# A second pair of output tiles by seven products, a visit moved ahead of a plain tile, and weight sums moved from GpSimd to VectorE

## The chip, the cores and the metric

The kernel runs on one core of one Trainium2 chip. The metric is the device time of one execution in microseconds (us). Engines are named as in the profile: PE is TensorE (matmuls; PEld its weight loads), DVE is VectorE, ACT is ScalarE, POOL is GpSimd, and SP is SyncE, which here only issues DMAs.

## The reference

Sigmoid attention without softmax, then a gated feed-forward block. Cut to what matters:

```python
# q, k, v: batch 8, heads 12, seq 448, head_dim 64
scores = scale * np.matmul(q, k.transpose(0, 1, 3, 2)) - np.log(S)
attn = 1.0 / (1.0 + np.exp(-scores))
x = np.matmul(attn, v)              # then (8 * 448, 12 * 64) = (3584, 768)
g = x @ w_gate                      # w_gate, w_val: (768, 1536)
silu = g * (1.0 / (1.0 + np.exp(-g)))
out = (silu * (x @ w_val)) @ w_out  # w_out: (1536, 768)
```

Inputs and output are float32; the kernel computes matmuls in 16-bit types with float32 accumulation.

## The kernel before

**Tiling.** Attention is cut into 24 blocks `n`, three for each batch and each of four heads. A block has seven chunks `c` of 64 keys for each head; `qk_tile` (L240) makes the scores of a chunk, `sig_tile` (L256, L259, on ACT) their sigmoid, and `pv` (L273) multiplies a whole block with v and gives two pieces `xT` of the feed-forward input. The feed-forward works on pairs of batches, `pb` 0 to 3. `ffn1(b, f)` (L314) makes 128 of the 1536 hidden columns for one batch, with the gate on ACT (L334) and DVE (L336, L340). In half of pair 2 and all of pair 3, `double` (L437) does two hidden columns of both batches at once by seven products of half-size blocks in place of eight (Strassen's scheme in Winograd's form). The second matmul gives seven output tiles of 128 rows for a pair.

**Output tiles, plain and grouped.** `ffn2(pb, m)` (L675) makes one output tile with 24 matmuls of 128x384; its two halves are evicted by ACT (L690) and DVE (L689). `ffn2_group(pb, g)` (L599) makes tiles `g` and `g + 3` together by seven products of six matmuls, 42 where two plain tiles need 48. It is a generator that stops after each product, in the order 1, 2, 6, 5, 7, 3, 4; the products alternate between the two banks of one PSUM tile and are evicted by DVE (L610, and L616, which adds to what is there), the first one by ACT (L623) when `act` is set. `ffn2_groups` runs several such generators in turn and calls one function of `extra` after each step.

**Sums.** The seven products need sums of blocks. `make_sums` takes row sums of the hidden tiles from a list (L532, DVE, 128x384). `w_sum(s, kind)` makes sums of `w_out`, eight in all (L498, DVE, 128x1152): kind 2 reads kind 3, and kind 4 reads kind 2. `fast_w(s, kind)` makes those of the first matmul's weights (L384): on DVE in one instruction when it is called from `extra` of a `double`, or on POOL in three of 128x384 when `early_w(2)` calls it, after POOL has made the sums of the last pair's input (L410 to L413). For `s` = 2 they are needed by the doubles from hidden column 6 on, for `s` = 3 from column 9 on.

**Order.** All is written in program order, and each engine runs its own instructions in that order. The list `units` holds `ffn1`, `double`, sums and output tiles with a planned length. `PACE` gives planned times for the attention blocks, and a visit (four or three chunks of a block; `attn_step`) is put ahead of the unit at which its time has come. After a visit, `plan` adds transfers: after chunk 4 of block `n` the casts of block `n + 2` (L191, POOL), their two DMA transposes (L198, SP), the load of its v (POOL) and the loads of q and k of block `n + 4` (SP). Stores of output tiles (L543) are issued by SP too, so all these stand in one queue; SP waits at the first whose data are not ready. POOL is often ahead of the program: it waits only for its own inputs.

**Memory.** Score tiles, gates, output tiles and groups take the four PSUM tiles of two banks in turn (`Banked`), whatever they are. Output tiles are staged in four buffers `osb`.

**Around the change.** At the end of pair 0 the order is: last gate `ffn1(1, 11)`, the last row sums, tile 6, the visit of block 8 (chunks 4 to 6), four `w_sum`, tile 0, three `w_sum`, tile 3, a visit of block 9, the group of tiles 1 and 4 (with the eighth `w_sum` after its second step), a visit, the group of tiles 2 and 5, a visit. In pair 3, six doubles follow each other with nothing between.

Of the kernel before, what the change touches and what calls it, by code (L numbers as in the profile page):

```python
# [13 lines left out]
MULT = mybir.AluOpType.mult  # L14
# [6 lines left out]
def kernel(  # L21
# [13 lines left out]
    B, H, S, D = q.shape  # L35
# [3 lines left out]
    NJ = H // 4  # L39
    NP = H // 2  # L40
    NF = DFF // 128
    NQ = B * NJ
    W2 = 2 * S
    LAST = B // 2 - 1
# [99 lines left out]
    def half_of(a):  # L144
        return a.rearrange("p a b s -> p (a b s)").bitcast(FP16)
# [160 lines left out]
    V, G = nc.vector, nc.gpsimd  # L306
# [51 lines left out]
    def fast_w(s, kind, i=None):  # L358

        js = slice(0, JT) if i is None else slice(i, i + 1)  # L360
        b11, b21 = wg16[s][:, 0::2][:, js], wg16[s][:, 1::2][:, js]
        b12, b22 = wv16[s][:, 0::2][:, js], wv16[s][:, 1::2][:, js]
        if (s, kind) not in gT:
            n = JT * FW * 128
            at = {3: 0, 2: 1, 4: 2}.get(kind)
            if kind == 1:
                t = wv16[s][:, 0::2]
            elif s == 0:
                t = half_of(stg_a)[:, at * n:(at + 1) * n]
            elif s == 1 and kind == 3:  # L370
                t = half_of(ramp_a)[:, 8 * FW * hw:8 * FW * hw + n]
            elif s == 1:
                t = pt_f[:, (at - 1) * n:at * n]
            elif s == 2:
                t = pt_f[:, (at + 2) * n:(at + 3) * n]
            else:
                t = osp.tile([128, DM], FP32, tag="osb", name=f"g{kind}").bitcast(FP16)[:, :n]
            gT[(s, kind)] = t if kind == 1 else t.rearrange("p (j n) -> p j n", j=JT)
        t = gT[(s, kind)][:, js]
        a, b, op = {  # L380
            3: (b22, b12, SUB), 1: (b12, b11, SUB), 2: (b22, gT.get((s, 1), gT[(s, kind)])[:, js], SUB),
            4: (b21, gT.get((s, 2), gT[(s, kind)])[:, js], SUB),
        }[kind]
        (V if i is None else G).tensor_tensor(out=t, in0=a, in1=b, op=op)  # L384
# [1 line left out]
    pt_f = pt_a.rearrange("p a b s -> p (a b s)")  # L386

    def early_w(s):
        for kind in (3, 1, 2, 4):
            for i in range(JT):  # L390
                fast_w(s, kind, i)

# [96 lines left out]
    def w_sum(s, kind):  # L489

        b11, b12 = wo16[2 * s][:, :, :hw], wo16[2 * s][:, :, hw:]
        b21, b22 = wo16[2 * s + 1][:, :, :hw], wo16[2 * s + 1][:, :, hw:]
        t = half_of(ramp_a)[:, len(wT) * FW * hw:(len(wT) + 1) * FW * hw].rearrange("p (f n) -> p f n", f=FW)
        wT[(kind, s)] = t
        a, b, op = {
            3: (b22, b12, SUB), 2: (wT.get((3, s)), b11, ADD), 1: (b12, b11, SUB), 4: (b21, wT.get((2, s)), SUB),
        }[kind]
        nc.vector.tensor_tensor(out=t, in0=a, in1=b, op=op)  # L498
# [35 lines left out]
    def store(engs, pb, m, osb, cols):  # L534

        for w in range(2):
            store_half(engs[w], pb, m, w, osb, cols)
# [119 lines left out]
        store((nc.sync, nc.scalar), *rows[1], oe, lo)  # L657

    def ffn2_groups(pb, gs, extra=()):
        gens = [ffn2_group(pb, g, len(gs) > 1) for g in gs]  # L660
        extra = list(extra)
        while gens:
            gens = [g for g in gens if next(g, g) is not g]
            if extra:
                extra.pop(0)()

    def ffn2(pb, m):
        D = Banked("o")

        head, tail = range(NF - 1), (NF - 1,)  # L670
        for half, fs in ((0, head), (1, head), (0, tail), (1, tail)):
            for f in fs:
                h = hT[(pb, f)].rearrange("p b s -> p (b s)")
                D.write(
                    nc.tensor.matmul(  # L675
                        out=D.t[:, half, :hw],
                        lhsT=h[:, m * 128:(m + 1) * 128],
                        rhs=wo16[f // FW][:, f % FW, half * hw:(half + 1) * hw],
                        start=(f == 0),
                        stop=(f == NF - 1),  # L680
                    ),
                    half,
                    uses=(pb, f),
                )
        osb = osp.tile([128, DM], FP32, tag="osb", name="osb")
        for half in range(2):
            o, i, by = osb[:, half * hw:(half + 1) * hw], D.t[:, half, :hw], 1.0 / hsc(pb)
            D.read(
                V.tensor_scalar(out=o, in0=i, scalar1=by, scalar2=None, op0=MULT) if half else  # L689
                nc.scalar.mul(out=o, in_=i, mul=by),  # L690
                half,
            )
        store((nc.sync, nc.sync), pb, m, osb, slice(0, DM))


    FU1, FU2, FU3, FU4 = 2.26, 3.9, 6.83, 7.85
    units = []
    f1_start, f1_end = {}, {}
    tt = 0.0
    for pb in range(B // 2):  # L700
        for b in (2 * pb, 2 * pb + 1):
            f1_start[b] = tt
            for f in range(NF):
                if f not in FAST.get(pb, ()):
                    if b or f > 2:
                        units.append((FU1, ffn1, (b, f)))
                    tt += FU1
            f1_end[b] = tt
        for f in FAST.get(pb, ())[::2]:
            extra = {  # L710
                (LAST - 1, 0): ((0, 4), (1, 2)), (LAST - 1, 2): ((1, 4),), (LAST, 0): ((3, 3), (3, 1)), (LAST, 2): ((3, 2), (3, 4)),
            }.get((pb, f), ())
            units.append((FU4, double, (pb, (f, f + 1), [lambda a=a: fast_w(*a) for a in extra])))
            tt += FU4
        o_units = [(0.0, make_sums, (99,))]
        if pb < LAST - 1:
            o_units.append((FU2, ffn2, (pb, C - 1)))
        if pb == 0:

            ts = [(0.0, w_sum, (s, kind)) for s in range(2) for kind in (3, 2, 1, 4)]  # L720
            o_units += ts[:4] + [(FU2, ffn2, (pb, 0))] + ts[4:7] + [(FU2, ffn2, (pb, 3))]
        ex = {(0, 1): (lambda: None, lambda: w_sum(1, 4)), (LAST - 1, 0): (keep_rest,)}
        gs = {0: ((1,), (2,)), LAST - 1: ((0, 1), (2,)), LAST: ((0, 1), (3,), (2,))}.get(pb, ((0,), (1,), (2,)))
        for g in gs:
            o_units.append((FU3 * len(g), ffn2_groups, (pb, g, ex.get((pb, g[0]), ()))))
        units += o_units
        tt += sum(u[0] for u in o_units)


    FIRST = f1_end[0] - 5.0  # L730
    PACE = ((2 * NJ, FIRST + 3.5), (3 * NJ, FIRST + 41.5), (3 * NJ + 2, FIRST + 60.5), (6 * NJ, f1_end[B - 5] - 1.0), (NQ, f1_end[B - 3] - 5.0))
    tiles = [(n, c) for n in range(NJ, NQ) for c in range(C)]
    visits = [tiles[:2], tiles[2:4]]
    for i in range(0, len(tiles), C):
# [2 lines left out]
    for grp in visits:  # L737
# [4 lines left out]
        else:  # L742
            at = n + (0.5 if c else 0.0)
            (n0, t0), (n1, t1) = [p for p in zip(PACE, PACE[1:]) if p[0][0] <= at][-1]
            vtime.append(t0 + (at - n0) / (n1 - n0) * (t1 - t0))
# [124 lines left out]
    early = [tile_of(0), tile_of(2)]  # L870
# [59 lines left out]
    for fn, args, how in seq:  # L930
# [28 lines left out]
        if fn is make_sums and hS and (LAST - 1, 4, FW - 1) in hS and (LAST, 3, 0) not in hS:  # L959
            G.tensor_copy(out=held[:, :1], in_=hS[(LAST - 1, 4, FW - 1)][:, :1])  # L960
            for j in range(NJ):
                for f in x_sums(LAST, j):
                    f()
            early_w(2)
# [32 lines left out]
```

## Time and profile before

| | |
|---|---|
| time, median of 4 runs | 404.52 us (404.25 to 407.78) |
| profiled execution, own time | 404.63 us |
| its span, first to last instruction | 402.9 us |
| granted TensorE clock, mean | 0.999 |
| PE busy | 391.7 us, 97% of the span |
| DVE, ACT, POOL busy | 270.0, 230.2, 104.4 us |
| plain output tiles (L675) | 4, 96 matmuls, 16.1 us on PE |
| sums on POOL for `s` = 2 (L384) | 12 instructions, 0.91 to 0.93 us each |

The page is of one execution. A line of the chain or of a timeline starts with the time from the start of the span and a length, both in us; "x" counts the instructions that were put together. In brackets stands how long the engine was idle before it, and what ended that. Lines are those of the kernel before. In the windows view, a stretch is followed by its length and the busy time of each engine in it.

### The profile page before, as it was taken

The numbers are of one execution on the slowest core, as the hardware profiler recorded it, in microseconds if no ns is written. First come the engines' busy times: TensorE is split into PE (matmuls) and PEld (weight loads), VectorE is DVE, ScalarE is ACT, GpSimd is POOL, SyncE is SP. The second block draws the span as 40 slices with busy tenths as digits, with TensorE's granted clock in tenths as the row PEclk, the third lists the DMA queues.
The fourth block names the chain that finished last, engine by engine and source line by source line (L and its number), as shares of the span: only waits on it lengthen the run. The fifth ranks groups of instructions, "written<-read, shape, count | busy, mean of one in ns | idle before, by whom it ended". The sixth has DMA issues, their size and how long they took to land.

```text
span 402.9 us, 8032 instructions
## 1 busy us (share of the span) xinstructions
PE 391.7 (97%) x3134; PEld 203.5 (51%) x3134; DVE 270.0 (67%) x509; ACT 230.2 (57%) x369; POOL 104.4 (26%) x146
## 2 busy tenths in 40 slices
PE   7799999999999999999999999999999999999995
PEld 3344545445555444444455554444555645555663
DVE  3637647798655555567774556888886588778753
ACT  5966885744444777777773547776654046756000
POOL 3628041352022232232200220000006950010700
PEclk9999999999999999999999999999999999999999
DMA  8999989998859997778716598000000530000055
GB/s 261 252 246 255 245 188 258 163 194 183 185 132 267 220 269 159 163 159 161 161 24 149 160 258 122 2 2 0 3 0 2 157 80 0 1 2 1 2 165 149
DMA packets 65286, 54.39 MB, mean 135 GB/s; under 512 B 35744, under 2 KB 61440, under 8 KB 65248
## 3 DMA queue, kind: packets, MB, share of 16 engines
q1 hardware_dynamic: 49744, 38.22, 37.8%
q0 software_dynamic: 15072, 15.34, 23.0%
q8 instruction: 24, 0.39, 0.4%
q10 hardware_dynamic: 432, 0.33, 0.3%
q14 instruction: 14, 0.11, 0.1%
HBM read 47.19 MB, written 11.01 MB: 144 GB/s over the span
## 4 chain that ended last, share of the span: by engine, by line
PE 92%; DMA 3%; DVE 2%; ACT 1%; issue 1%; SPq 0%; POOL 0%; DVEq 0%; ACTq 0%
PE ps_D L314 35%; PE ps_D L599 20%; PE ps_D L437 16%; PE ps_D L240 8%; PE ps_D L273 8%; PE ps_D L675 4%; DMA v<-in_v_dram 2%; DMA st<-in_q_dram 1%; DVE g L384 1%; PE ps_D L210 0%; DVE t L336 0%; DVE xT L288 0%; DVE xT L293 0%; ACT snap L447 0%; ACT s L334 0%
## 5 line engine op out<-in xcount | busy, mean ns | idle before, releaser
L259 ACT ACTIVATE pt_a<-ps_D 128x896 f16<-128x896 f32 x148 | 127.2, 918 | 54.8 <-PE ps_D L240 49.3
L314 PE MATMUL ps_D<-xT,wg 128*128 128x448 f16 x360 | 79.4, 353 | 0.6 <-DVE t L336 0.5
L314 PE MATMUL ps_D<-xT,wv 128*128 128x448 f16 x360 | 78.9, 352 | 0.0
L191 POOL CAST c<-stg_a 128x896 bf16<-128x896 f32 x40 | 37.5, 946 | 133.3 <-DMA stg_a<-in_q_dram 125.6
L336 DVE TENSOR_TENSOR t<-ps_D,s 128x448 f16<-128x448 f32 x60 | 37.4, 624 | 41.5 <-ACT s L334 40.5
L314 PEld LDWEIGHTS <-wg 128*128 128x128 f16 x360 | 32.3, 98 | 39.4 <-issue 13.6
L314 PEld LDWEIGHTS <-wv 128*128 128x128 f16 x360 | 35.1, 98 | 33.0 <-issue 0.4
L334 ACT ACTIVATE s<-ps_D 128x448 f16<-128x448 f32 x60 | 33.0, 550 | 26.5 <-PE ps_D L314 26.5
L240 PE MATMUL ps_D<-T,T 64*64 64x448 bf16 x644 | 44.1, 357 | 2.1 <-DVE T L216 1.0
L447 ACT ACTIVATE snap<-ps_D 128x448 f32<-128x448 f32 x54 | 28.0, 542 | 26.3 <-PE ps_D L437 24.7
L340 DVE SCALAR_TENSOR_TENSOR hT<-ps_D,t 128x448 f16<-128x448 f32 x60 | 37.5, 625 | 6.3
L273 PE MATMUL ps_D<-pt_a,v 64*64 64x448 f16 x672 | 35.9, 349 | 0.7 <-DMA v<-in_v_dram 0.7
L610 DVE TENSOR_SCALAR osb<-ps_D 128x384 f32<-128x384 f32 x43 | 24.0, 558 | 18.5 <-PE ps_D L599 17.8
L599 PEld LDWEIGHTS <-S 128*128 128x128 f16 x264 | 25.8, 98 | 17.1
L599 PE MATMUL ps_D<-ramp_a,S 128*128 128x384 f16 x198 | 33.6, 326 | 0.0
L616 DVE SCALAR_TENSOR_TENSOR osb<-ps_D,osb 128x384 f32<-128x384 f32 x36 | 20.0, 557 | 13.8 <-PE ps_D L599 13.8
L240 PEld LDWEIGHTS <-T 64*64 64x64 bf16 x644 | 14.9, 105 | 24.4 <-issue 17.9
L599 PEld LDWEIGHTS <-hT 128*128 128x128 f16 x204 | 19.6, 98 | 14.4 <-issue 1.8
L273 PEld LDWEIGHTS <-v 64*64 64x64 f16 x672 | 19.4, 107 | 13.5 <-DMA v<-in_v_dram 1.1
L288 DVE CAST xT<-ps_D 128x448 f16<-128x448 f32 x21 | 13.1, 625 | 18.9 <-PE ps_D L273 17.1
L293 DVE CAST xT<-ps_D 64x448 f16<-64x448 f32 x37 | 23.0, 622 | 0.8
L437 PE MATMUL ps_D<-xS,wv 128*128 128x448 f16 x108 | 23.4, 352 | 0.0
(110 smaller groups left out, 442.9 us busy)
## 6 DMA issues: line engine op xcount, KB each, us to landing
out_dram<-osb SPq DMA_DIRECT2D x52, 192.0 KB, 3.1
stg_a<-in_q_dram SPq DMA_DIRECT2D x18, 448.0 KB, 4.8
stg_a<-in_k_dram SPq DMA_DIRECT2D x18, 448.0 KB, 5.3
v<-in_v_dram POOLq DMA_DIRECT2D x24, 224.0 KB, 6.0
wg<-in_moe_w_gate_dram POOLq DMA_DIRECT2D x4, 576.0 KB, 12.4
wv<-in_moe_w_val_dram POOLq DMA_DIRECT2D x4, 576.0 KB, 12.7
wo<-in_moe_w_out_dram POOLq DMA_DIRECT2D x4, 576.0 KB, 9.5
stg_a<-in_q_dram POOLq DMA_DIRECT2D x3, 448.0 KB, 14.8
```

Source lines behind the costliest of these rows:

```text
L191: eng.tensor_copy(out=t.rearrange("p c h d -> p h c d"), in_=st.rearrange("p h (c d) -> p h c d", c=C))
L240: nc.tensor.matmul(out=sc[w * 64:(w + 1) * 64, h2, :S], lhsT=kt[r, w * 64:(w + 1) * 64], rhs=qt[r, :, w * 64:(w + 1) * 64], start=True, st ...
L259: nc.scalar.activation(out=pt, in_=sc[:, :, :S], func=SIGM, bias=sbias, scale=qkscale)
L273: nc.tensor.matmul(out=P[g:g + 64, h2, :S], lhsT=vt[r, h2, c * D:(c + 1) * D], rhs=pt[r, h2, :], start=(c == 0), stop=(c == C - 1),)
L314: nc.tensor.matmul(out=D.t[:, i, :S], lhsT=(wg16, wv16)[i][f // FW][:, pr, cs], rhs=xT[(b, pr)], start=(pr == 0), stop=(pr == NP - 1),),
L334: D.read(nc.scalar.activation(out=s16, in_=D.t[:, 0, :S], func=SIGM), 0)
L336: D.read(nc.vector.tensor_tensor(out=t1, in0=D.t[:, 0, :S], in1=s16, op=MULT), 0)
L340: nc.vector.scalar_tensor_tensor(out=hT[(b // 2, f)][:, b % 2, :], in0=D.t[:, 1, :S], scalar=hsc(b // 2), in1=t1, op0=MULT, op1=MULT),
L437: nc.tensor.matmul(out=D.t[:, bank, :S], lhsT=W(f, j), rhs=X(j), start=(start and j == 0), stop=(stop and j == JT - 1), skip_group_check=True,
L447: D.read(nc.scalar.mul(out=o, in_=D.t[:, bank, :S], mul=scale), bank)
L599: nc.tensor.matmul(out=D.t[:, bank, :hw], lhsT=l, rhs=B_(i), start=(first and i == 0), stop=(i == HF - 1), skip_group_check=True,),
L610: nc.vector.tensor_scalar(out=o, in0=D.t[:, bank, :hw], scalar1=1.0 / hsc(pb), scalar2=None, op0=MULT), bank
```

## The change

Tiles 0 and 3 of pair 0 become a group, run after tile 6 with its first eviction on ACT. Both halves of the plain tile 6 of pair 0 are evicted by ACT. Six of the eight `w_sum` stand before that group, four of them ahead of tile 6, and the other two are called after its third and fourth step. `PACE` gets two more points, so that the visit of block 8 (chunks 4 to 6) comes right after the last gate, ahead of the row sums and of tile 6; its other points are moved a little, and the order of all other visits stays the same. On the first weights, `early_w(2)` makes kinds 3 and 1 on POOL and no longer kinds 2 and 4; these go to DVE, as extras of the first and second double of pair 3. The extras for `s` = 3 move back: (3,3) from the first double to the second, (3,1) and (3,2) to the third, (3,4) to the fourth.

```diff
     def early_w(s):
-        for kind in (3, 1, 2, 4):
+        for kind in (3, 1):
             for i in range(JT):
                 fast_w(s, kind, i)
...
     def ffn2_groups(pb, gs, extra=()):
-        gens = [ffn2_group(pb, g, len(gs) > 1) for g in gs]
+        gens = [ffn2_group(pb, g, len(gs) > 1 or (pb, g) == (0, 0)) for g in gs]
...
-                V.tensor_scalar(out=o, in0=i, scalar1=by, scalar2=None, op0=MULT) if half else
+                V.tensor_scalar(out=o, in0=i, scalar1=by, scalar2=None, op0=MULT) if half and pb else
                 nc.scalar.mul(out=o, in_=i, mul=by),
...
             extra = {
-                (LAST - 1, 0): ((0, 4), (1, 2)), (LAST - 1, 2): ((1, 4),), (LAST, 0): ((3, 3), (3, 1)), (LAST, 2): ((3, 2), (3, 4)),
+                (LAST - 1, 0): ((0, 4), (1, 2)), (LAST - 1, 2): ((1, 4),), (LAST, 0): ((2, 2),),
+                (LAST, 2): ((2, 4), (3, 3)), (LAST, 4): ((3, 1), (3, 2)), (LAST, 6): ((3, 4),),
             }.get((pb, f), ())
...
         if pb == 0:
-
-            ts = [(0.0, w_sum, (s, kind)) for s in range(2) for kind in (3, 2, 1, 4)]
-            o_units += ts[:4] + [(FU2, ffn2, (pb, 0))] + ts[4:7] + [(FU2, ffn2, (pb, 3))]
-        ex = {(0, 1): (lambda: None, lambda: w_sum(1, 4)), (LAST - 1, 0): (keep_rest,)}
-        gs = {0: ((1,), (2,)), LAST - 1: ((0, 1), (2,)), LAST: ((0, 1), (3,), (2,))}.get(pb, ((0,), (1,), (2,)))
+            early = [(0.0, w_sum, a) for a in ((0, 3), (0, 2), (1, 3), (1, 2), (0, 1), (1, 1))]
+            o_units[1:1] = early[:4]
+            o_units += early[4:]
+        skip = lambda: None
+        ex = {
+            (0, 0): (skip, skip, lambda: w_sum(0, 4), lambda: w_sum(1, 4)), (LAST - 1, 0): (keep_rest,),
+        }
+        gs = {LAST - 1: ((0, 1), (2,)), LAST: ((0, 1), (3,), (2,))}.get(pb, ((0,), (1,), (2,)))
...
-    PACE = ((2 * NJ, FIRST + 3.5), (3 * NJ, FIRST + 41.5), (3 * NJ + 2, FIRST + 60.5), (6 * NJ, f1_end[B - 5] - 1.0), (NQ, f1_end[B - 3] - 5.0))
+    PACE = ((2 * NJ, FIRST + 3.5), (3 * NJ - 1, FIRST + 28.9), (3 * NJ - 0.5, f1_end[1] - 0.1), (3 * NJ, FIRST + 41.5), (3 * NJ + 2, FIRST + 59.5), (6 * NJ, f1_end[B - 5] - 1.0), (NQ, f1_end[B - 3] - 5.5))
```

## The prediction

> **What bounds the kernel now.** I read the page first (busy shares, the chain that ended last), then the chain in order of time at the two places that the change touches, then the timelines of VectorE (DVE), GpSimd (POOL) and SyncE (SP) there.
>
> ```profile
> PE 391.7 (97%) x3134; PEld 203.5 (51%) x3134; DVE 270.0 (67%) x509; ACT 230.2 (57%) x369; POOL 104.4 (26%) x146
> ...
> PE 92%; DMA 3%; DVE 2%; ACT 1%; issue 1%; SPq 0%; POOL 0%; DVEq 0%; ACTq 0%
> ```
>
> TensorE (PE) is busy for 97% of the span and holds 92% of the chain: a matmul taken away counts fully, and so does a wait put in front of one. The rest is read in two places. The first is the end of pair 0 (start, length, what):
>
> ```profile
> 97.46 3.90 PE ps_D L675 x24
> 101.36 0.69 PE ps_D L240 x12
> 102.06 7.91 PE ps_D L675 x48
> ...
> 112.17 6.93 PE ps_D L599 x42
> ```
>
> L675 is the plain product: tile 6 from 97.46, tiles 0 and 3 from 102.06. L599 is a pair of tiles made by seven products. The chain here is PE alone: 48 matmuls cost 7.91 us, 42 cost 6.93. The second place is the first double of the last pair:
>
> ```profile
> 325.86 2.95 DVE g L384
> ...
> 329.51 0.63 DVE v L473
> 330.14 0.04 issue
> 330.18 1.86 PE ps_D L437 x9
> ```
>
> Here the chain leaves PE: a weight sum on DVE (L384) takes 2.95 us, the eviction L473 is late behind it, and PE waits for that.
>
> **The change, part by part.** *1, the group.* Tiles 0 and 3 lose 48 matmuls and gain 42: 6.93 - 7.91 = **-0.98 us**, on the path.
>
> *2, the sums ahead of the group.* In the built order DVE runs the last row sums (L532), then six of the eight weight sums L498, (0,3), (0,2), (1,3), (1,2), (0,1), (1,1), and only then L616, the eviction of the group's second product. Their pace:
>
> ```profile
> 102.24 0.75 DVE L498 TENSOR_TENSOR ramp_a<-wo,wo 128x1152 f16<-128x1152 f16 x1
> 103.02 0.76 DVE L498 TENSOR_TENSOR ramp_a<-ramp_a,wo 128x1152 f16<-128x1152 f16 x1
> 103.70 0.75 DVE L498 TENSOR_TENSOR ramp_a<-wo 128x1152 f16<-128x1152 f16 x1
> ```
>
> A sum that reads its predecessor starts 0.78 after it, another 0.67 after. The row sums end at 100.38 (99.76 + 0.62 in the same view), as they will; six sums from 100.3 take 0.78 + 0.67 + 0.78 + 0.67 + 0.67 between their starts, so the last runs 103.9 to 104.6, and L616 (0.56) ends at 105.1. On PE the visit (0.69) now comes at 97.46, tile 6 (3.90) after it, the group at 102.05. Its fourth product in order writes the bank that L616 reads; it comes after 18 of 42 matmuls, 2.97 us on, at 105.0, and waits until 105.15: **+0.15**. The third product, at 104.0, needs sum (1,2), ready at 103.3. So visit and tile 6, 4.6 us of PE, are the cover of these sums, and it is used up: whatever delays DVE further between 98.4 and 104.6 reaches PE whole. Sums (0,4) and (1,4) run inside the group, some 0.5 us before its last product needs them.
>
> *3, the visit ahead of tile 6.* Its score tiles take PSUM tiles whose readers end by 96.7; tile 6 takes that of the last gate, read until 98.50 in the bank that it writes second: nothing waits. The visit carries two casts and a v load (POOL), two transposes and two loads (SP). POOL's order stays. On SP the transposes of block 10 and the loads of block 12 pass tile 6's two stores. SP, and then the casts on POOL that these loads release:
>
> ```profile
> 91.11 1.19 SPq L179 DMA_DIRECT2D stg_a<-in_k_dram  x1
> 102.35 1.19 SPq L543 DMA_DIRECT2D out_dram<-osb  x2
> 103.64 2.67 SPq L198 DMA_TRANSPOSE T<-c  x2
> 106.37 0.58 SPq L179 DMA_DIRECT2D stg_a<-in_q_dram  x1
> ```
>
> ```profile
> 110.44 0.93 POOL L191 CAST c<-stg_a 128x896 bf16<-128x896 f32 x1 [11.21 <-DMA stg_a<-in_q_dram]
> 111.97 0.94 POOL L191 CAST c<-stg_a 128x896 bf16<-128x896 f32 x1 [0.60 <-POOL c L191]
> ```
>
> SP stands from 92.3 to 102.35 at a store that waits for an eviction. With that store behind them, the transposes (cast by 90.5) go at 92.4, the loads at 95.1 and 95.8. From load to cast took 4.07 and 4.97 us here (issued 106.37 and 107.00), 5.18 and 6.53 for the two issued at 90.47 and 91.11. So the casts of block 12 move to 99.2-100.3 and 100.8-102.3, **into the sums of part 2**. What that costs, other rows show, POOL's and DVE's:
>
> ```profile
> 86.61 3.84 POOL L191 CAST c<-stg_a 128x896 bf16<-128x896 f32 x4
> ```
>
> ```profile
> 86.77 1.01 DVE L532 TENSOR_TENSOR S<-hT,S 128x384 f16<-128x384 f16 x1
> 87.70 1.08 DVE L532 TENSOR_TENSOR S<-hT 128x384 f16<-128x384 f16 x1
> ```
>
> Alone such a row sum takes 0.35. The five beside casts, from 71.7 to 90.7, took 1.43, 0.71, 1.01, 1.08 and 0.70: 0.64 lost in the mean, each to one cast. Bounds for one cast: nothing (the sum at 98.42 beside the cast of 97.64 took 0.37), and 1.08. A gain is excluded, as a cast gives DVE nothing. I take the mean, since these rows have the same cast and the same kind of sum: 2 x 0.64 = **+1.28**; ends 0 and 2.16.
>
> The Trainium skill (SBUF — State Buffer, "Who interferes with whom") says that a DVE instruction with two inputs in SBUF contends with a GpSimd instruction that reads SBUF, and that the one that issues second is blocked until the first has finished. That speaks against putting these sums under casts. By it a cast could cost its whole 0.93, the sum of the case then being 0.6 higher, near 405.0. The trace goes beyond the rule: the L384 of 325.86 was overtaken by two POOL sums that started after it.
>
> *4, two kinds of sums from POOL to DVE.* POOL's run of L384 (0.88 each) ends six instructions earlier, at about 322.9 instead of 328.2. In the first double DVE then has one sum of 0.75 with POOL idle in place of 2.95 + 0.75, and L473 is on time. The first double took 8.54 us on PE from start to start (322.77 to 331.31), the next 7.95 (to 339.26): **-0.59**; ends -0.43 (PE's bare idle time there) and -0.60. The second double keeps two sums. The third gets two (1.47 from their rows) ahead of its row sums: these end at 345.2 in place of 343.74, L473 starts at 345.13 instead of 344.80 and ends at 345.75, and its product comes at 346.07: hidden by 0.3; if that cover is gone it costs up to 0.3. The fourth double gets one sum, where DVE idled 0.67.
>
> *5, small parts.* Evictions: the group adds six on DVE (0.56 each) and takes three away, in a stretch with 3.8 us of DVE idle in 12.5; tile 6's second half goes to ScalarE, whose three evictions (0.49 each) end by 103.7, ahead of the third product at 104.0. The stores stay 14. Block 11's transposes still stand behind the first group's stores, at 120, and are read at 136. All at nothing.
>
> *Sum:* -0.98 + 0.15 + 1.28 - 0.59 = -0.14 us. The profiled execution took 404.63 (span 402.9 and 1.7 around it): 404.49; it stood 0.11 above the median of 404.52, so 404.4 for a median.
>
> **The rivals.** *A, the casts cost nothing:* they miss the sums (load 12 lands later than any row says), or DVE, which has its sums queued, holds POOL up instead. For it: the sum at 98.42. Against: six weight sums and six row sums leave no hole from 98.4 to 104.6, and both casts are due inside. Sum: -0.98 + 0.15 - 0.59 = -1.42: **403.1**. With one cast alone, 403.7.
>
> *B, slower: POOL keeps DVE out in a run.* At 325.86 a DVE sum of 0.75 waited through the rest of three POOL sums in a row, losing 2.19. If both casts and the v issue behind them run back to back (0.93 + 0.94 + 0.72), DVE loses 2.59: -0.98 + 0.15 + 2.59 - 0.59 = +1.17: **405.7**. It takes hold from a loss of 1.42 on, and needs the two landings within 0.9 of each other; against it, the last two pairs of casts lay 1.53 and 1.99 apart.
>
> *C, the change doesn't do what it says in the last pair:* the late row is the third double's, part 4 gives 0.3 back: 404.7.
>
> **How the numbers follow.** Forecast 0.50, its own range by the bounds of the cast from 0.35 each to 1.08 each: 403.8 to 405.3. A 0.30, B 0.15, C 0.05. The range takes in A with its bounds and the upper end of the forecast, up to B's edge: 403.0 to 405.5. One per cent, 4.0 us, is about what a measurement of this kernel can tell from no change; no case comes near it: faster 0.02, same 0.96, slower 0.02.
>
> **What would show it.** Right: POOL casts between 99 and 104, an L498 or L532 there of over 1 us, a gap on PE before the fourth product of the group (near 105) of 1 to 2 us, and visit (9,0) on PE near 110.4 instead of 109.96; in the last pair no PE wait at 330 and L384 at 0.75. Wrong: L498 all at 0.75 and visit (9,0) near 109.1 (A), or one L498 of 3 us (B); PE waiting for L473 in the third double (C); any wait in blocks 9 to 12 that was not there.

## The result

The changed kernel takes 405.49 us in the median of 54 runs (half of them between 404.9 and 406.4), beside 404.40 in the median of 78 runs of the kernel before (half between 404.1 and 404.7). The ratio of the times is 1.003, with an interval of 1.002 to 1.0039: 1.1 us slower, where 0.1 us faster was forecast. The profiled execution took 405.01 us, with a span of 403.2: only 0.38 more than the profiled execution before, and 0.5 below its own median. That gap turned out to matter.

The head of the page after, with the busy time of the engines and the shares of the chain that ended last:

```profile
PE 390.3 (97%) x3128; PEld 202.7 (50%) x3128; DVE 272.8 (68%) x514; ACT 230.3 (57%) x369; POOL 100.1 (25%) x140
...
PE 90%; DVE 3%; DMA 3%; ACT 1%; issue 1%; SPq 0%; POOL 0%; DVEq 0%; ACTq 0%
```

PE has six matmuls fewer, as planned, and is busy for 1.4 us less, but it holds 90% of the chain in place of 92%, and DVE 3% in place of 2%: the time that PE gave up went to waits for DVE. The timeline of all engines after shows where. These are rows from the second of SyncE's transposes of block 10 to the visit of block 9 on PE (start, length, what; in brackets the idle time of that engine before the row, and what ended it):

```profile
93.17 3.30 SPq L198 DMA_TRANSPOSE T<-c  x1
...
96.52 0.57 SPq L179 DMA_DIRECT2D stg_a<-in_q_dram  x1
97.15 0.46 SPq L179 DMA_DIRECT2D stg_a<-in_k_dram  x1
...
100.54 1.01 POOL L191 CAST c<-stg_a 128x896 bf16<-128x896 f32 x1 [1.42 <-DMA stg_a<-in_q_dram]
100.67 1.49 DVE L498 TENSOR_TENSOR ramp_a<-wo,wo 128x1152 f16<-128x1152 f16 x1
...
102.14 2.11 PE L599 MATMUL ps_D<-wo,hT 128*128 128x384 f16 x12
...
103.09 1.32 POOL L191 CAST c<-stg_a 128x896 bf16<-128x896 f32 x1 [1.55 <-DMA stg_a<-in_k_dram]
103.65 1.37 DVE L498 TENSOR_TENSOR ramp_a<-ramp_a,wo 128x1152 f16<-128x1152 f16 x1
...
105.07 0.65 PE L599 MATMUL ps_D<-ramp_a,S 128*128 128x384 f16 x3 [0.33 <-DVE ramp_a L498]
106.28 0.55 DVE L616 SCALAR_TENSOR_TENSOR osb<-ps_D,osb 128x384 f32<-128x384 f32 x1
106.88 2.11 PE L599 MATMUL ps_D<-ramp_a,S 128*128 128x384 f16 x12 [1.16 <-DVE osb L616]
110.87 0.57 PE L240 MATMUL ps_D<-T,T 64*64 64x448 bf16 x8
```

Read it from top to bottom. The transposes and loads go 10 to 12 us earlier than before. The two casts that the loads release fall on two weight sums (L498), which take 1.49 and 1.37 in place of 0.75. PE waits twice, first for a sum and then for L616, which stands behind the sums. From the group's first matmul to the visit after it PE needs 110.87 - 102.14 = 8.73 us, where 42 matmuls take 6.93: a wait of 1.80 (the idle times in brackets are shorter, since they count the modelled ends of matmuls that run into the gap). 42 matmuls and this wait cost 0.82 more than the 48 of two plain tiles (7.91).

In the last pair the trace after looks as predicted (DVE's timeline):

```profile
326.84 0.75 DVE L384 TENSOR_TENSOR pt_a<-wv 128x1152 f16<-128x1152 f16 x1
329.30 1.16 DVE L473 SCALAR_TENSOR_TENSOR v<-ps_D,snap 128x448 f16<-128x448 f32 x2 [1.71 <-ACT snap L447]
```

The sum of 2.95 us is gone and L473 waits for ACT, not for a sum. So the two profiles differ by about +0.9 at the end of pair 0 and -0.6 in the last pair, which gives their 0.3 to 0.4. The medians differ by 1.1. The -0.6 is most of what is missing.

### The profile page after: what moved, and what is told of

The parts are those of the page before. It is cut to its first block, busy times and chain, and to the rows that moved or that the text cites. A ratio compares the mean times of both kernels' runs of the same rounds, so it can differ in the third digit from the quotient of the medians.

```text
span 403.2 us, 8014 instructions
## 1 busy us (share of the span) xinstructions
PE 390.3 (97%) x3128; PEld 202.7 (50%) x3128; DVE 272.8 (68%) x514; ACT 230.3 (57%) x369; POOL 100.1 (25%) x140
## 4 chain that ended last, share of the span: by engine, by line
PE 90%; DVE 3%; DMA 3%; ACT 1%; issue 1%; SPq 0%; POOL 0%; DVEq 0%; ACTq 0%
PE ps_D L314 34%; PE ps_D L599 21%; PE ps_D L437 18%; PE ps_D L240 8%; PE ps_D L273 8%; DMA v<-in_v_dram 2%; DVE ramp_a L498 1%; PE ps_D L675 1%; DMA st<-in_q_dram 1%; ACT pt_a L259 1%; DVE t L336 0%; PE ps_D L210 0%; DVE S L532 0%; ACT s L334 0%; DVE xT L288 0%
## 5 line engine op out<-in xcount | busy, mean ns | idle before, releaser
L610 DVE TENSOR_SCALAR osb<-ps_D 128x384 f32<-128x384 f32 x46 | 25.6, 557 | 19.6 <-PE ps_D L599 19.4
L599 PE MATMUL ps_D<-ramp_a,S 128*128 128x384 f16 x216 | 37.1, 326 | 1.5 <-DVE osb L616 1.2
L599 PEld LDWEIGHTS <-S 128*128 128x128 f16 x288 | 28.2, 98 | 20.4 <-issue 1.9
L616 DVE SCALAR_TENSOR_TENSOR osb<-ps_D,osb 128x384 f32<-128x384 f32 x39 | 21.6, 557 | 14.0 <-PE ps_D L599 14.0
L599 PEld LDWEIGHTS <-hT 128*128 128x128 f16 x222 | 21.3, 98 | 15.6 <-issue 1.8
L599 PE MATMUL ps_D<-wo,hT 128*128 128x384 f16 x144 | 25.1, 326 | 0.0
```

Of the source, the lines that this page charges most:

```text
L599: nc.tensor.matmul(out=D.t[:, bank, :hw], lhsT=l, rhs=B_(i), start=(first and i == 0), stop=(i == HF - 1), skip_group_check=True,),
L610: nc.vector.tensor_scalar(out=o, in0=D.t[:, bank, :hw], scalar1=1.0 / hsc(pb), scalar2=None, op0=MULT), bank
```

## The experiments

The theory on trial was that of the prediction: the two casts of block 12 fall on the sums, and each takes from DVE what a collision takes. Its rivals were the rest of part 2 (too many sums ahead of L616 even without casts), the moved DMA traffic, and the moved visit by itself. Each time below is held against runs of the kernel before that were taken beside it; these have medians of 404.17, 404.51 and 404.15, so that a difference of 0.3 between times of two sets tells little. The ratios and their intervals are taken over all runs and not from the medians, and can differ by some tenths of a per cent from the quotient of the two medians.

**Take the casts away, in two ways.** The first kernel keeps the changed order of PE and DVE, but issues the transfers of the visit of block 8 after tile 6, as before:

```diff
+    if (n, c) == (8, 4): late.append((act, of))
+    else: act(of)
...
+    if fn is ffn2 and args == (0, C - 1):
+        for act, of in late: act(of)
```

> The changed kernel with the visit still ahead of tile 6, but the transfers that the visit carries (casts and transposes of block 10, v load, loads of block 12) written after tile 6 and its stores, as before the change. Theory (the casts of block 12 meet the weight sums and hold VectorE up): loads of block 12 at 106, their casts at 110 to 113, all L498 at 0.75 us, PE waits at most 0.2 us before the fourth product of the group, visit of block 9 on PE near 109.3; time 1.4 us under the kernel before, 403.0, and the runs no wider apart than those of the kernel before. Rival 1 (six sums ahead of the group are too long for their cover even alone): the wait of 1.7 us stays, 405.5. Rival 2 (the moved transposes and loads themselves cost, by DMA traffic): also near 403.0, so this run doesn't tell it from the theory; the next does.

Measured: 403.97 beside 404.17, ratio 0.9968 (0.9941 to 0.9994). The group with its casts (and the old last pair, which will turn out to make some 0.1) took 405.40 beside the same runs of the kernel before, 1.4 more. The forecast was 403.0; most of the difference is a wait that stays without casts and a gain in the last pair that does not come, both below. The timeline of the kernel with late transfers, rows of all engines in the same place:

```profile
100.98 0.75 DVE L498 TENSOR_TENSOR ramp_a<-wo,wo 128x1152 f16<-128x1152 f16 x1
...
102.27 2.11 PE L599 MATMUL ps_D<-wo,hT 128*128 128x384 f16 x12
...
105.85 2.11 PE L599 MATMUL ps_D<-ramp_a,S 128*128 128x384 f16 x12 [0.49 <-DVE osb L616]
...
109.84 0.57 PE L240 MATMUL ps_D<-T,T 64*64 64x448 bf16 x8
...
111.22 0.93 POOL L191 CAST c<-stg_a 128x896 bf16<-128x896 f32 x1 [13.92 <-DMA stg_a<-in_q_dram]
```

The first cast of block 12 is at 111.22, behind the group; every weight sum has its 0.75; PE needs 109.84 - 102.27 = 7.57, a wait of 0.64. So 1.16 of PE's wait goes with the casts. In the changed kernel's own rows the two sums lost 0.74 and 0.61, 1.35 together, and 1.80 - 1.35 leaves 0.45; here the wait without casts is 0.64, since a row sum ahead of the last gate had been hit by another cast (1.08 at 94.68) and DVE came 0.2 later to the rest. Either way more is left than the 0.15 predicted.

The second kernel leaves all DMAs of the change where they are, and makes POOL hold the casts back by a copy of one column of a late weight sum into a spare tile:

```diff
+def hold_w(i): G.tensor_copy(out=held[:, :1], in_=wT[(4, 1)][:, 0, :1])
+plan[(10, 4)] = ((hold_w, 0),) + plan[(10, 4)]
```

> The changed kernel with its transfers where it has them, and one GpSimd instruction more: ahead of the casts of block 12 it reads one column of the eighth weight sum, so that these casts start only when the sums are done (near 107.5). Theory: as the kernel with late transfers, 1.4 us under the kernel before, 403.0; loads of block 12 still issued at 96 to 97. Rival 1: 405.5. Rival 2 (DMA traffic): as the changed kernel, 405.5, with its wide spread.

Measured: 403.93, ratio 0.9971 (0.9938 to 1.0004). Its SyncE and POOL timeline:

```profile
97.03 0.57 SPq L179 DMA_DIRECT2D stg_a<-in_q_dram  x1
...
108.24 0.18 POOL L910 CAST held<-ramp_a 128x1 bf16<-128x1 f16 x1 [8.64 <-DVE ramp_a L498]
108.36 1.80 POOL L191 CAST c<-stg_a 128x896 bf16<-128x896 f32 x2
```

The load of block 12 is as early as in the changed kernel (97.03 beside 96.52), and the time is that of the first experiment. The DMA traffic costs nothing that can be seen; the casts do. PE's wait here is 1.05, because an earlier cast, the second of block 11, met a row sum (0.95 in place of 0.35): 0.45 and 0.60.

**Give it more casts.** In this kernel one cast of block 12 is made three times over, so that four casts stand where two stood:

```diff
+        for _ in range(3 if (n, which) == (12, 0) else 1):
             eng.tensor_copy(...)
```

> The changed kernel with the first cast of block 12 written three times in a row (same input, same output), so that the suspected cost is doubled: four casts beside the sums instead of two. Theory: VectorE loses 0.6 to 0.75 us more for each cast that finds it in the sums; with the first cast near 100.5 all four do, and the fourth product comes 1.2 to 1.5 us later than in the changed kernel: 406.8. Rival 2 (DMA traffic sets the loss): as the changed kernel, 405.5.

Measured: 407.78 beside 404.51, ratio 1.0065 (1.0038 to 1.0093). POOL's timeline, then PE's (one added line moves the numbers of lines by one):

```profile
99.99 4.33 POOL L192 CAST c<-stg_a 128x896 bf16<-128x896 f32 x4 [1.62 <-DMA stg_a<-in_q_dram]
```

```profile
104.99 0.66 PE L600 MATMUL ps_D<-ramp_a,S 128*128 128x384 f16 x3 [0.64 <-DVE ramp_a L499]
...
106.45 0.65 PE L600 MATMUL ps_D<-ramp_a,S 128*128 128x384 f16 x3 [0.80 <-DVE ramp_a L499]
...
108.25 2.11 PE L600 MATMUL ps_D<-ramp_a,S 128*128 128x384 f16 x12 [1.16 <-DVE osb L617]
```

Four casts hit two row sums (1.04 and 0.97) and two weight sums (1.48 and 1.37). PE's wait is 3.1 (102.23 to 112.24, less 6.93). The four sums lost 0.68, 0.61, 0.73 and 0.61, together 2.63, which with 0.45 is this wait. In this place POOL did not keep DVE out through its run of casts: each sum was held by one cast and came in before the next. The profiled execution took 406.39, 1.4 above that of the changed kernel for 1.3 more of wait; the median is another 1.4 above it, which this trace does not cover.

**The visit alone.** The kernel before, with only the two points of `PACE` that move the visit of block 8 ahead:

```diff
-    PACE = ((2 * NJ, FIRST + 3.5), (3 * NJ, FIRST + 41.5), ...
+    PACE = ((2 * NJ, FIRST + 3.5), (3 * NJ - 1, FIRST + 28.9), (3 * NJ - 0.5, f1_end[1] - 0.1), (3 * NJ, FIRST + 41.5), ...
```

> The kernel before with only the visit of block 8 moved ahead of tile 6, its transfers with it. Theory: the casts of block 12 meet the weight sums here too, but these have until 112 (two plain tiles of PE work stand between), so an L498 or two takes 1.4 us and nothing waits: same as before, 404.4, within 0.2. Rival (moving the visit with its transfers costs by itself, whatever the group): 405.2.

Measured: 404.74 beside 404.51, ratio 1.0014 (0.9985 to 1.0042). Its DVE and PE timeline:

```profile
99.75 1.07 DVE L532 TENSOR_TENSOR S<-S,hT 128x384 f16<-128x384 f16 x1
```

```profile
97.98 11.87 PE L675 MATMUL ps_D<-wo,hT 128*128 128x384 f16 x72
109.79 0.57 PE L240 MATMUL ps_D<-T,T 64*64 64x448 bf16 x8
```

A cast meets a sum here too, a row sum (1.07) and not a weight sum as expected, and PE does not notice: 72 matmuls of three plain tiles stand between, and 109.79 - 97.98 = 11.81 us is what they took in the kernel before (3.90 + 7.91). The time alone would not exclude the rival's 0.8 us, since the interval reaches up to 1.7 us; the trace shows no wait for it. The moved visit makes the collision, and the group takes away its cover.

**Each half of the change by itself.** One kernel has only the last pair's part (`early_w` with kinds 3 and 1, and the new extras), the other everything else:

```diff
 # last pair only: the kernel before, with
-        for kind in (3, 1, 2, 4):
+        for kind in (3, 1):
...
 # group only: the changed kernel, with
-        for kind in (3, 1):
+        for kind in (3, 1, 2, 4):
```

> The kernel before with only the move of the weight sums of the last pair (two kinds from GpSimd to VectorE, extras of the doubles moved back). Theory: the first double of pair 3 loses its wait, 8.54 us become 7.95, and nothing else changes: 0.59 us under the kernel before, 403.8. Rival (the freed time is lost again, in the third double): 404.4.

> The changed kernel without that move in the last pair: pair 0 as changed, pair 3 as before. Theory: the profiled loss of 0.83 us of pair 0 stands alone, 0.6 us over the changed kernel: 405.2 if the profiled execution is typical, 406.1 if the median of the changed kernel (405.5) is; spread as wide as that of the changed kernel. Rival (the spread and part of the loss come from pair 3): 405.0 or less with the spread of the kernel before.

Measured: the last pair alone 404.37, ratio 0.9994 (0.9958 to 1.0029); the group alone 405.40, ratio 1.0027 (0.9994 to 1.0061). The group carries the loss. The last pair's trace is in order (L384 0.75 at 326.18, no wait on PE, 7.94 for the first double and for the third), and yet its median shows no gain. 404.37 is the rival's time, but not by the rival's reason, and the interval, from 1.7 us below to 1.2 above, would not exclude the 0.59. The traces tell more, first that of the group's kernel, which has the old last pair. DVE's timeline there, then PE's:

```profile
326.92 1.17 DVE L384 TENSOR_TENSOR g<-wv 128x1152 f16<-128x1152 f16 x1
328.12 1.35 DVE L384 TENSOR_TENSOR wv<-wv,wg 128x1152 f16<-128x1152 f16 x1
```

```profile
330.65 1.30 PE L437 MATMUL ps_D<-stg_a 128*128 128x448 f16 x6
331.78 2.43 PE L437 MATMUL ps_D<-xT,wg 128*128 128x448 f16 x12
```

Same code, other outcome: two sums of 1.17 and 1.35, together 2.5 us in place of 3.7, and no idle time in front of the product that waited 0.43 in the profile before. The first double takes 331.78 - 323.84 = 7.94, as long as any other.

**The changed kernel once more**, for a second profile of it:

> The changed kernel once more, to set its second profile and its times beside these on one chip. Theory: time 405.5 and wide spread, since the landing of the loads of block 12 differs between executions and with it the share of the two casts that lies under the sums; its profile again shows both casts beside the sums and the visit of block 9 on PE 0.8 to 1.6 us later than in the kernel before. Rival (the median is above the profile for a reason outside pair 0): the wait in pair 0 is as in the first profile and a second place has lost time.

Measured: 405.47 beside 404.51, ratio 1.0028 (1.0002 to 1.0054), and this time a profiled execution of 405.45, at the median. POOL's timeline, then PE's:

```profile
102.46 2.44 POOL L191 CAST c<-stg_a 128x896 bf16<-128x896 f32 x2 [2.61 <-DMA stg_a<-in_q_dram]
```

```profile
105.56 0.65 PE L599 MATMUL ps_D<-ramp_a,S 128*128 128x384 f16 x3 [0.73 <-DVE ramp_a L498]
...
107.37 2.11 PE L599 MATMUL ps_D<-ramp_a,S 128*128 128x384 f16 x12 [1.16 <-DVE osb L616]
...
111.36 0.57 PE L240 MATMUL ps_D<-T,T 64*64 64x448 bf16 x8
```

The casts came 1.9 us later than in the first profile and still inside the sums, and the second cast of block 11 hit a row sum as well (0.75 in place of 0.35). PE's wait is 2.20 (102.23 to 111.36, less 6.93). So the first profile after was a mild execution, as the profile before was a bad one in the last pair.

**A version without the wait.** The first experiment, with two of the six row sums (kind 4) run behind L616, since only the group's sixth product in order reads them. The edit also gives the last gate no sums to run, so that the four that stay are sorted:

```diff
+            (0, 0): (skip, lambda: make_sums(99), lambda: w_sum(0, 4), lambda: w_sum(1, 4)),
...
+            budget[args] = 0 if args == (1, NF - 1) else 3 if ahead[0] else 0 if ahead[1] == 4 else 2
...
+    def first_sums(most):
+        sumq.sort(key=lambda s: s[3] % 3 if s[3] < 4 else 3)
+        make_sums(len([s for s in sumq if s[3] < 4]))
```

> The kernel with late transfers, and two of the six row sums ahead of the group (kind 4, which only the sixth product reads) put behind L616 instead. Theory: without casts a wait of 0.6 us before the fourth product was left, because six row sums and six weight sums take 6.4 us on VectorE; two row sums less (0.8 us) end it. Visit of block 9 on PE 6.9 to 7.0 us after the start of the group; time 0.6 us under the kernel with late transfers, about 2 under the kernel before: 402.6. Rival (the wait there is set by something else than the sums): as with late transfers, 403.2 to 404.0.

Measured: 403.48 beside 404.51, ratio 0.9978 (0.995 to 1.0007). Its PE timeline:

```profile
102.15 2.11 PE L603 MATMUL ps_D<-wo,hT 128*128 128x384 f16 x12
104.10 3.09 PE L603 MATMUL ps_D<-ramp_a,S 128*128 128x384 f16 x18
...
109.30 0.57 PE L240 MATMUL ps_D<-T,T 64*64 64x448 bf16 x8
```

No idle time stands in brackets in front of any product, and it takes 7.15 from the first matmul to the visit; the 0.22 above 6.93 lies in front of the last two products, and what it waits for stays open. The time is in the range of the rival, 403.2 to 404.0, and 0.9 above the forecast, but the rival's reason is not what the trace shows: with fewer sums ahead of L616 the wait in front of the fourth product is gone. It was run again, beside the same kernel with the last pair as before:

> The kernel with late transfers and two row sums behind L616 once more, beside the next one and beside the kernel before. Theory: 403.4 to 403.6, 1.0 us under the kernel before, most runs within 0.3 of each other.

> The same, but the weight sums of the last pair as in the kernel before (kinds 2 and 4 for doubles 6 to 8 on GpSimd, two sums in the first double). It shows the worth of that move alone, beside a kernel with narrow spread. Theory: the wait in the first double of pair 3 comes back, 0.6 us: 404.0 to 404.2. Rival (the move in the last pair saves time in the profile only): as the kernel beside it, 403.5.

Measured: 403.43 and 403.55 beside 404.15, ratios 0.9991 (0.997 to 1.0012) and 0.9987 (0.9966 to 1.0008). Twice 0.7 to 1.0 us below the kernel before and 2.0 below the changed one in the median; the ratios' intervals against the kernel before just take in 1, so that gain is likely and not settled. The last pair's part makes 0.1 here, inside the spread, where the forecast was 0.6. In the trace with the old last pair DVE's two sums took 1.21 and 1.35, and PE did not wait there either.

## Why the prediction was wrong

Two steps failed. The gain of 0.59 in the last pair was booked from a single event and did not come, and the rest that the sums leave without casts was put at 0.15 and measures 0.45 to 0.64. Part by part:

*Part 1, the group (-0.98): right.* The version without the wait takes 109.30 - 102.15 = 7.15 where two plain tiles take 7.91, and 0.2 of that is a remaining wait.

*Part 3, the casts (+1.28): right in kind, and in size with some luck.* They were forecast at 99.2 to 100.3 and 100.8 to 102.3 and came at 100.54 and 103.09 in one execution, at 102.46 and right behind it in the other; later than the forecast, and still inside the sums, which lost 1.35. The 0.64 for each cast was a mean of unlike rows, and not each of one cast: the sum of 0.71 stood beside POOL's issue of a v load (85.87, 0.74 us), and that of 1.43 began under another issue ahead of its cast. What a collision costs follows a simpler pattern, which the last section gives. The prediction also took it that the second cast of block 11 would miss the row sums, as in the trace before; it cost the first of them 0.40 in the second profile, 0.60 in the kernel with casts held back and 0.13 in that with the group only. Taking the two casts of block 12 away brings 1.4 in the medians (405.40 to 403.97). Rival A's case does not happen, and made to happen it gives 403.9 to 404.0 and not 403.1, because of the next two points.

*Part 2, the sums ahead of the group (+0.15): mis-sized, it measures 0.45 to 0.64.* The step that failed is the end of the row sums at 100.38, "as they will". DVE's row sums before, then after:

```profile
98.42 0.37 DVE L532 TENSOR_TENSOR S<-hT,hT 128x384 f16<-128x384 f16 x1
98.82 0.36 DVE L532 TENSOR_TENSOR S<-S,hT 128x384 f16<-128x384 f16 x1
99.10 0.35 DVE L532 TENSOR_TENSOR S<-hT,hT 128x384 f16<-128x384 f16 x1
99.48 0.36 DVE L532 TENSOR_TENSOR S<-S,hT 128x384 f16<-128x384 f16 x1
99.76 0.62 DVE L532 TENSOR_TENSOR S<-hT,S 128x384 f16<-128x384 f16 x2
```

```profile
98.56 0.35 DVE L532 TENSOR_TENSOR S<-hT,hT 128x384 f16<-128x384 f16 x1
98.94 0.36 DVE L532 TENSOR_TENSOR S<-S,hT 128x384 f16<-128x384 f16 x1
99.34 0.36 DVE L532 TENSOR_TENSOR S<-hT,S 128x384 f16<-128x384 f16 x1
99.61 0.35 DVE L532 TENSOR_TENSOR S<-hT,hT 128x384 f16<-128x384 f16 x1
100.00 0.36 DVE L532 TENSOR_TENSOR S<-S,hT 128x384 f16<-128x384 f16 x1
100.39 0.36 DVE L532 TENSOR_TENSOR S<-hT,S 128x384 f16<-128x384 f16 x1
```

The prediction took over the pace of the trace before. There the last gate runs two of the six (its `budget`) and `make_sums` sorts the other four, so that two of the six read the sum just before them. A visit now follows the last gate directly, and for that `budget` gives the gate three sums: it runs three of the six unsorted and `make_sums` the other three, two chains in which four of the six read the sum just before them. Such a sum starts 0.38 to 0.40 after its predecessor, another 0.27 or 0.28. From the first row sum to the first weight sum it takes 98.56 to 100.67 after, 2.11 where the prediction had 1.88 (98.42 to 100.3), and nothing covers the 0.23. The rest is DVE's later arrival, 0.05 against PE in the first profile after (98.56 and 102.14 where 98.42 and 102.05 were forecast), and 0.2 more in the kernel with late transfers, where a cast hit a sum still further ahead. Moving two sums behind L616 ended the wait (7.57 to 7.15 on PE).

*Part 4, the last pair (-0.59): the mechanism is there, the gain is not.* The wait that the change removes stands in one of four traces of the old code, the profile before. The other three are of the kernel with the group only, the last experiment and the kernel with only the visit moved: DVE's first sum takes 1.17, 1.21 and 1.16 beside POOL's run, and the double takes 7.94 in all three. The medians agree: 404.37 beside 404.17, and 403.43 beside 403.55. The term should have been near 0, but it was bounded by -0.43 and -0.60 from one event that does not come out alike each time. What decides it stays open; it is not which engine comes first, since POOL's run starts 0.34 us ahead of DVE's sum in the profile before and 0.33 to 0.36 ahead in the three others. Rival C (part 4 loses) did not happen: the third double's L473 started at 345.50 and nothing waited for it.

*Part 5 at nothing:* right. In the first profile after, PE waits at the end of pair 0 for a weight sum and for L616 alone.

*The sum, mended:* -0.98 + 1.80 to 2.20 + 0 = +0.8 to +1.2, beside +1.1 measured. Rival B's time, 405.7, is close to that, but not by its mechanism: at the group no trace has a DVE sum that was kept out for longer than one cast, not even by four casts in a row. At another place, in the first profile after too, it does happen, as the last section shows.

What stays open: why the changed kernel's runs lie further apart (404.9 to 406.4 in their middle half, 404.1 to 404.7 before), and the kernel with three casts in place of one far above its profile. The two profiles after, with waits of 1.80 and 2.20 and first casts 1.9 us apart, would fit landing times of the loads that differ between executions. A sum at the group that is held through two casts, as rival B had it, would make an execution longer still; no trace shows one there.

## What to carry to other kernels

A product that gets shorter takes cover away from whatever runs beside it: before a plain tile is replaced, list what stood hidden under it, with its price, and leave the evicting engine slack for the worst of it or move that work. A wait that comes from two engines meeting is one draw from a set: before a gain is booked for removing it, see it in a second execution, or carry zero as its other end. Work that only later products read belongs behind the eviction that the next product waits for.

## What was unexpected of the hardware

DVE and POOL do not take turns by a fixed order. In the profile before, one DVE sum took 2.95 us and waited through three POOL sums, two of which started after it. POOL's timeline there:

```profile
325.52 2.67 POOL L384 TENSOR_TENSOR pt_a<-wg,pt_a 128x384 f16<-128x384 f16 x3
```

In the kernel with only the group, the same three POOL sums let DVE in between and took longer themselves:

```profile
326.56 3.69 POOL L384 TENSOR_TENSOR pt_a<-wg,pt_a 128x384 f16<-128x384 f16 x3
```

Casts do the same. Four of them in a row stand between 84 and 91 us in every kernel here. In the profile before they alternate with three row sums (0.71, 1.01 and 1.08, the first beside the v load issued ahead of them); in the changed kernel the first sum there took 1.79 in place of 0.35, and in the kernel with only the last pair changed, where that stretch is as in the kernel before, it was held through three casts (DVE, then POOL):

```profile
86.26 2.87 DVE L532 TENSOR_TENSOR S<-S,hT 128x384 f16<-128x384 f16 x1
```

```profile
86.22 3.69 POOL L191 CAST c<-stg_a 128x896 bf16<-128x896 f32 x4
```

PE had other work then, and nothing waited.

The Trainium skill (SBUF — State Buffer, "Who interferes with whom") has the first of the two that issues hold the other off for its whole length. For a single meeting the rows here agree, in price too. In the trace after, the first cast ends at 101.55 and the sum that started under it at 102.16, the second cast at 104.41 and its sum at 105.02: each sum of 0.75 ends 0.61 after its cast, so that it lost what was left of the cast when it started, less 0.14. The casts were themselves stretched, to 1.01 and 1.32, where they started while a sum ran. The rows do not agree in order once several POOL instructions follow each other: the sums of 2.95 and 2.87 were overtaken by POOL instructions that started after them.
